# Rebuilding the first batch of a fused attention and Fourier-mixing kernel: order of transposes, loads and folds, and one mixing product over all channels

## The chip, the cores and the metric

The kernel runs on one core of one Trainium2 chip. The metric is the device time of one launch in microseconds (us). Before the change it took 1139.79 us, the median of three runs (1139.76 to 1141.58 us); the profiled execution spans 1140.0 us from its first to its last instruction. Where a moment is given below, it is counted from the start of that span. The engines are TensorE (PE; PEld is its weight load), VectorE (DVE), ScalarE (ACT), GpSimd (POOL) and SyncE (SP), which here only issues transfers.

## What is computed

There are 8 batches, 8 heads, 576 tokens and a head width of 64. Attention is local to chunks of 64 tokens. Its output, laid out as 576 x 512 for each batch, goes through a Fourier mix over tokens and channels, a normalization and a two-layer MLP (512 to 2048 to 512).

```python
def _attn_ref(q, k, v):                       # 8 x 8 x 576 x 64, chunk = 64
    scores = scale * np.matmul(q_c, k_c.transpose(0, 1, 2, 4, 3))
    scores = scores - np.max(scores, axis=-1, keepdims=True)
    attn = np.exp(scores)
    attn = attn / (np.sum(attn, axis=-1, keepdims=True) + 1e-09)
    return np.matmul(attn, v_c)

def _moe_ref(x, w_ch1, w_ch2):                # x: 8 x 576 x 512
    X = np.fft.fft(x, axis=1)
    X = np.fft.fft(X, axis=2)
    u = x + np.real(X).astype(np.float32)
    mu = np.mean(u, axis=-1, keepdims=True)
    var = np.mean((u - mu) ** 2, axis=-1, keepdims=True)
    un = (u - mu) / np.sqrt(var + 1e-06)
    return u + np.maximum(un @ w_ch1, 0.0) @ w_ch2
```

The two weight matrices arrive as float64 and are turned into float32 on the chip, piece by piece (32 pieces of 128 x 512).

## The kernel before

A batch's nine chunks make four tiles of 128 tokens and half a tile. "LO" tiles hold chunks from the front, "HI" tiles chunks from the back in mirrored order, and "RE" (rest) tiles hold the middle chunks of two batches. Token n and token 576 - n share their Fourier factors, so a LO and a HI tile are **folded**: their sums and differences are taken over tokens and then over channels, which quarters the Fourier products. For this the LO tiles are shifted by one row across tile borders (`shift`). The Fourier transform is then two matrix products with cosine and sine tables: `z` over the tokens, `mix` over the channels.

The first batch has nothing before it to hide behind, so it has its own code. The MLP of group 0 can start when the four tiles of batch 0 are normalized and transposed; from then on the MLPs of all groups follow each other on PE, and the next batches' attention, the rounding of the weights (`round_weight`) and a conversion of the second weight matrix (`keep2`) are woven in between the MLP's steps.

The order of the first batch's work (cut):

```python
def attention_early():
    def ready(n):
        for i in range(NM):                   # NM = 2
            if n == at[LO, 0, i]: shift_early(i)
            if n == at[HI, 0, i]: fold(0, i)  # on VectorE
        if n == at[LO, 0, 0]: fold(0, NM)     # the rest tile, on GpSimd
        if n + 3 > hi: load_v(n + 3)
    att_T(lo)                                 # q, k transposed by PE, copied by ACT
    for n in range(lo, hi + 1):               # 5 tiles: RE, LO 0, LO 1, HI 0, HI 1
        att_S(n)                              # scores on PE; max, subtract (DVE); exp (ACT)
        if n > lo:
            att_V(n - 1)                      # product with v, scaled by DVE
            ready(n - 1)
        if n < hi:
            att_T(n + 1)
        yield
        att_P(n)                              # probabilities transposed; sums, reciprocal
        yield
    att_V(hi)
    ready(hi)
    yield
```

The fold of one pair, the rounding of one piece, and the main program's beginning (all cut):

```python
def fold(b, i):
    eng = nc.vector if b < 2 and (b, i) != (0, NM) else nc.gpsimd
    ...                                       # for a pair: sum of two tiles 128x512,
    ...                                       # four adds or subtracts 128x256, two small copies

def round_weight(i):
    if i < len(pieces):                       # first half of piece i
        nc.vector.tensor_scalar(wi, hi, 0x000FFFFF, None, ALU.bitwise_and)
        nc.scalar.activation(out=w, in_=wi, func=ACTF.Copy, scale=2.0 ** -20, bias=1.0)
        nc.vector.tensor_scalar(p, hi, 0x7FF00000, None, ALU.bitwise_and)
        nc.scalar.activation(out=p, in_=p, func=ACTF.Relu, scale=-1.0, bias=top[:, 0:1])
        nc.scalar.activation(out=p, in_=p, func=ACTF.Relu, scale=-8.0, bias=top[:, 1:2])
    if 0 < i <= len(pieces):                  # second half of piece i - 1
        nc.vector.scalar_tensor_tensor(w, lo, 2.0 ** -52, w, ALU.mult, ALU.add)
        nc.vector.scalar_tensor_tensor(p, hi, 0x80000000, p, ALU.bitwise_and, ALU.bitwise_or)
        nc.vector.tensor_tensor(out=w, in0=w, in1=p.bitcast(FP32), op=ALU.mult)

# main
for n in range(3): load(n); load_v(n)         # q, k and v of tiles 0 to 2
for n in range(3, first[1]): load(n)
for n in range(3, first[1]): load_v(n)
for i in range(len(spaces)): load_weight(i)   # 7 pieces of the weights
for step, _ in enumerate(attention_early()):
    if step == 0:
        load_tables()                         # issued by GpSimd
        load_dim_tables()
    if step == 6:
        turn_tables()                         # copies on GpSimd
    keep_warm(1)                              # idle matmuls, 2 instructions each
keep_warm(5)
for step, _ in enumerate(fourier(0)):
    for _ in range((2, 1, 0)[step]):
        round_next()
...
for g in range(NG):                           # the MLPs
    for _ in mlp(g):
        ...                                   # due steps of the next batch's attention
        if not heavy:
            round_next()
            if t <= 4 or t % 4 == 0:
                round_next()
        for _ in range(2 if n_w <= len(pieces) else 3):
            if n_w > N_LAST + 2 and n_conv < 5 or n_w > len(pieces):
                n_conv += 1
                next(conv2, None)             # a step of keep2, mostly one DVE operation
```

In `fourier(0)` the token products are taken for one pair of quarters after the other, each over both tile pairs and the rest; the channel product `mix` covers half of the channels and its mirror half is made by two VectorE operations a tile (`both`) from a copy that ACT makes.

Of the kernel before, what the change touches and what calls it, by code (L numbers as in the profile page):

```python
# [16 lines left out]
def kernel(  # L17
# [94 lines left out]

    LO, HI, RE = "lo", "hi", "rest"
    tiles, first = [], []
    for b in range(B):
        first.append(len(tiles))
        if b % 2 == 0:
            tiles.append((RE, b, 0))
        tiles += [(what, b, i) for what in (LO, HI) for i in range(NM)]
# [37 lines left out]
    es, rs, pT = {}, {}, {}  # L157
# [3 lines left out]
    dims = [start[:, d0 + o:d0 + o + n_] for o, n_ in ((0, HM + 1), (HM + 1, HM - 1), (2 * HM, HM + 1), (3 * HM + 1, HM - 1))]  # L161
# [53 lines left out]
    def load_tables():  # L215
# [5 lines left out]
        for c in range(2 * NM):  # L221
            (i, r0), (j, p0) = divmod(c * CH, 128), divmod((NC - 1 - c) * CH, 128)
            nc.gpsimd.dma_start(out=t[r0:r0 + CH, i], in_=seq_tab[p0:p0 + CH, j])
        for r0 in (0, CH):
            nc.gpsimd.dma_start(out=t[r0:r0 + 1, NM], in_=seq_tab[0:1, 0])
            nc.gpsimd.dma_start(out=t[r0 + 1:r0 + CH, NM], in_=seq_tab[1:CH, NM])

    def load_dim_tables():
        nc.gpsimd.dma_start(out=dims[0], in_=dim_tab[:, 0, 0:HM + 1])
        nc.gpsimd.dma_start(out=dims[1], in_=dim_tab[:, 2, 1:HM])  # L230
        nc.gpsimd.dma_start(out=dims[2][0:1], in_=dim_tab[0:1, 1, 0:HM + 1])
        nc.gpsimd.dma_start(out=dims[3][0:1], in_=dim_tab[0:1, 3, 1:HM])

    def turn_tables():
        t = start[:, 0:(NM + 1) * 2 * NQ]
        a, b = tk.rearrange("p i r f -> p (i r) f"), t.rearrange("p (i f) -> p i f", f=NQ)
        for c in range(2 * NM):
            nc.gpsimd.tensor_copy(a[:, :, c * CH:(c + 1) * CH], b[:, :, (c + 1) * CH:c * CH:-1])
        nc.gpsimd.tensor_copy(a[:, :, NL:NL + 1], b[:, :, 0:1])
        nc.gpsimd.tensor_copy(a[:, :, NL + 1:NQ], b[:, :, NL + 1:NQ])  # L240
        nc.gpsimd.memset(cx[:, 0:HQ + 1], 0.0)
        nc.gpsimd.tensor_copy(ce, dims[0][:, ::2])
        nc.gpsimd.tensor_copy(co, dims[0][:, 1::2])
        nc.gpsimd.tensor_copy(so, dims[1][:, ::2])
        nc.gpsimd.tensor_copy(so[0:1], dims[3][0:1, ::2])
        nc.gpsimd.tensor_copy(cx[:, HQ + 1:HM], dims[1][:, 1::2])
        nc.gpsimd.memset(cx[0:1, HQ + 1:HM], 0.0)
        nc.gpsimd.tensor_copy(cx[0:1, 0:HQ + 1], dims[2][0:1, ::2])
# [58 lines left out]
    def att_T(n):  # L307
# [24 lines left out]
        if low and n == at[LO, 0, 1]:  # L332
# [12 lines left out]
    def att_S(n):  # L345
        a, b = qT.pop(n), kT.pop(n)
        sc = ps_a.tile([128, 2, 512], FP32, tag="att", name="sc")
        for j in range(NJ):
            for e in range(2):
                for c in range(2):  # L350
# [7 lines left out]
                    )  # L358
        s4 = sc[:, :, 0:NJ * CH].rearrange("p e (j k) -> p e j k", j=NJ)
# [24 lines left out]
    def att_V(n):  # L384
# [35 lines left out]
        if kind(n) == HI:  # L420
            nc.gpsimd.tensor_copy(x[:, 0:1], x[:, DM:DM + 1])
# [3 lines left out]
    def shift_early(i):  # L425

        lows = [xt(at[LO, 0, j])[:, 0:DM] for j in range(NM)]
        rest = xt(rests[0])[0:1, 0:DM]
        if i == 0:
            nc.gpsimd.tensor_copy(first_rest[CH:CH + 1, 0:DM], rest)  # L430
            nc.gpsimd.tensor_copy(rest, lows[0][0:1])
            nc.gpsimd.tensor_copy(lows[0][0:1], lows[0][CH:CH + 1])
        else:
            nc.scalar.copy(lows[0][CH:CH + 1], lows[1][0:1])
            nc.scalar.copy(lows[1][0:1], lows[1][CH:CH + 1])
            nc.scalar.copy(lows[1][CH:CH + 1], first_rest[CH:CH + 1, 0:DM])
# [15 lines left out]
    def fold(b, i):  # L452

        eng = nc.vector if b < 2 and (b, i) != (0, NM) else nc.gpsimd
        two = one_p.tile([128, 2 * (HM + 1)], FP32, tag="two", name="two")
        if i < NM:
# [3 lines left out]
            nc.gpsimd.memset(s[:, DM:DM + 1], 0.0)  # L460
# [27 lines left out]
    def attention_early():  # L488
# [3 lines left out]
        def ready(n):  # L492
            for i in range(NM):
                if n == at[LO, 0, i]:
                    shift_early(i)
                if n == at[HI, 0, i]:
                    fold(0, i)
            if n == at[LO, 0, 0]:
                fold(0, NM)
            if n + 3 > hi:  # L500
# [3 lines left out]
        for n in range(lo, hi + 1):  # L504
            att_S(n)
            if n > lo:
                att_V(n - 1)
                ready(n - 1)
            if n < hi:
                att_T(n + 1)  # L510
            yield
            att_P(n)
            yield
# [626 lines left out]
```

## Time and profile before

| | before |
|---|---|
| time, median of 3 | 1139.79 us |
| PE busy | 1093.8 us (96% of the span) |
| DVE busy | 599.2 us (53%) |
| ACT busy | 290.3 us (25%) |
| POOL busy | 274.3 us (24%) |
| read from HBM | 166.96 MB |
| first matmul of the first MLP | 65.10 us |

Busy times overlap, so they do not add up to the span. "L303" is line 303 of the kernel. In a line of the timeline the first number is the start and the second the duration; in brackets stands how long the engine sat idle before it, and after the arrow whose work ended that idle time. In the view by windows, each engine's busy time stands with the number of its instructions, then the TensorE clock granted as a share of full speed, the busy share of the 16 DMA engines and the GB/s that they moved. The matmuls are float32, and each one that the program asks for shows as two instructions.

### The profile page before, as it was taken

How to read it: one execution, taken by the hardware profiler on the slowest of the kernel's cores; microseconds unless marked ns; L12 is line 12 of the kernel's file. 1: busy time of each engine (PE TensorE's matmuls, PEld its weight loads, DVE VectorE, ACT ScalarE, POOL GpSimd, SP SyncE). 2: the span in 40 equal slices, each digit the busy share in tenths (PEclk: the TensorE clock that was granted, in tenths of full speed). 3: DMA queues.
4: the chain of work that ended last, by engine and by line, in shares of the span. 5: the costliest groups of instructions: out<-in, count | busy, mean ns of one | idle time of the engine just before them, and what ended most of it. 6: DMA issues, size and time to landing. Idle time of an engine off the chain costs nothing. (4 is left out here: it accounts for less than half of the span.)

```text
span 1140.0 us, 18688 instructions
## 1 busy us (share of the span) xinstructions
PE 1093.8 (96%) x7040; PEld 846.3 (74%) x7040; DVE 599.2 (53%) x1241; ACT 290.3 (25%) x711; POOL 274.3 (24%) x406
## 2 busy tenths in 40 slices
PE   5789998999999999999999999899999999999998
PEld 4544444445888888778888888788888888888887
DVE  4699978524356445563556365654555434423521
ACT  3577652121202221222113211321032202201210
POOL 4100101336400531043305140063015400130140
PEclk9999998999999999999999999999999999999999
DMA  9737652787556725773466546662664246446332
GB/s 172 221 96 210 177 175 72 225 262 234 211 168 188 234 96 181 230 198 118 165 209 173 176 140 203 179 206 111 187 203 125 84 161 197 128 145 214 94 108 77
DMA packets 150123, 192.47 MB, mean 169 GB/s; under 512 B 68820, under 2 KB 106713, under 8 KB 142865
## 3 DMA queue, kind: packets, MB, share of 16 engines
q1 hardware_dynamic: 147184, 189.57, 54.7%
q0 software_dynamic: 704, 1.17, 0.5%
q8 instruction: 56, 0.92, 0.3%
q10 hardware_dynamic: 2144, 0.52, 0.3%
q14 instruction: 35, 0.28, 0.1%
HBM read 166.96 MB, written 24.12 MB: 168 GB/s over the span
## 5 line engine op out<-in xcount | busy, mean ns | idle before, releaser
L791 POOL TENSOR_TENSOR h<-h 128x256 f32<-128x256 f32 x64 | 55.4, 871 | 415.6 <-PE pb L885 303.3
L932 PE MATMUL pa<-wb,h 128*128 128x256 f32 x512 | 116.1, 381 | 0.0
L932 PE MATMUL pb<-wb,h 128*128 128x256 f32 x512 | 115.0, 381 | 0.0
L885 PE MATMUL pb<-unT,wa 128*128 128x256 f32 x448 | 106.7, 381 | 4.4 <-DVE wa L894 4.4
L885 PE MATMUL pb<-wa 128*128 128x256 f32 x448 | 107.1, 382 | 0.8 <-DMA wa<-s 0.6
L885 PE MATMUL pa<-unT,wa 128*128 128x256 f32 x448 | 107.8, 383 | 0.0
L932 PEld LDWEIGHTS pa<-wb,h 128*128 128x128 f32 x512 | 95.8, 190 | 14.6 <-issue 1.6
L932 PEld LDWEIGHTS pb<-wb,h 128*128 128x128 f32 x512 | 95.8, 190 | 12.9
L885 PEld LDWEIGHTS pb<-unT,wa 128*128 128x128 f32 x448 | 84.2, 190 | 18.9 <-DVE wa L894 7.6
L885 PEld LDWEIGHTS pb<-wa 128*128 128x128 f32 x448 | 83.5, 190 | 13.7 <-DVE wa L892 1.2
L885 PEld LDWEIGHTS pa<-unT,wa 128*128 128x128 f32 x448 | 83.2, 190 | 11.6
L900 ACT ACTIVATE h<-pa 128x256 f32<-128x256 f32 x56 | 21.5, 384 | 176.2 <-PE pa L885 143.2
L839 PE MATMUL dn<-wb,h 128*128 128x512 f32 x128 | 60.6, 623 | 1.9 <-ACT h L809 1.9
L801 PE MATMUL up<-unT,wa 128*128 128x512 f32 x128 | 58.0, 599 | 1.7 <-ACT h L809 0.9
L892 DVE TENSOR_TENSOR wa<-pa,wa 128x256 f32<-128x256 f32 x56 | 23.8, 425 | 66.5 <-PE pa L885 62.9
L932 PE MATMUL pa<-wb,yall 128*128 128x256 f32 x256 | 58.2, 382 | 0.0
L885 PE MATMUL pa<-wa 128*128 128x256 f32 x224 | 54.0, 384 | 3.8 <-ACT wa L890 3.8
L818 PE MATMUL up<-unT,wa 128*128 128x512 f32 x128 | 57.5, 598 | 0.0
L932 PE MATMUL pb<-wb,yall 128*128 128x256 f32 x256 | 57.1, 380 | 0.0
L932 PE MATMUL pb<-wb 128*128 128x256 f32 x256 | 56.6, 379 | 0.0
L932 PEld LDWEIGHTS pb<-wb 128*128 128x128 f32 x256 | 48.2, 190 | 6.3
L636 POOL TENSOR_TENSOR xall<-y,xall 128x513 f32<-128x513 f32 x14 | 21.3, 1522 | 131.1 <-DVE y L630 131.1
(211 smaller groups left out, 1698.5 us busy)
## 6 DMA issues: line engine op xcount, KB each, us to landing
wb<-s SPq DMA_DIRECT2D x56, 1024.0 KB
wa<-s SPq DMA_DIRECT2D x196, 256.0 KB
xall<-in_moe_w_ch_dram SPq DMA_DIRECT2D x22, 512.0 KB
q<-in_q_dram SPq DMA_DIRECT2D x96, 112.0 KB
k<-in_k_dram SPq DMA_DIRECT2D x96, 112.0 KB
v<-in_v_dram SPq DMA_DIRECT2D x132, 64.0 KB
yall<-in_moe_w_ch_dram SPq DMA_DIRECT2D x10, 512.0 KB
s<-wb SPq DMA_DIRECT2D x20, 256.0 KB
```

Source lines behind the costliest of these rows:

```text
L636: eng.tensor_tensor(out=x[:, 0:w], in0=y[:, 0:w], in1=x[:, 0:w], op=ALU.add)
L791: nc.gpsimd.tensor_tensor(out=h1[:, m, hi], in0=h1[:, m, lo], in1=h1[:, m, hi], op=ALU.subtract)
L801: nc.tensor.matmul(out=up, lhsT=w1[:, kk, m * 128:(m + 1) * 128], rhs=unT[:, kk], start=(kk == 0), stop=(kk == KD - 1),)
L818: nc.tensor.matmul(out=up, lhsT=w1[:, kk, m * 128:(m + 1) * 128], rhs=unT[:, kk], start=(kk == 0), stop=(kk == KD - 1),)
L839: nc.tensor.matmul(out=dn, lhsT=h1[:, m, s * 128:(s + 1) * 128], rhs=w2[:, m, :], start=(m == 0), stop=(m == KF - 1),)
L885: nc.tensor.matmul(out=dst, lhsT=w[:, kk, r], rhs=rhs[o][:, kk], start=(o in (0, 2) and kk == 0), stop=(kk == 1), skip_group_check=True,)
L892: nc.vector.tensor_tensor(out=b, in0=dst, in1=a, op=ALU.add)
L900: nc.scalar.activation(out=h1[:, m, lo], in_=dst, func=ACTF.Relu)
L932: nc.tensor.matmul(out=dst, lhsT=lhs[:, m], rhs=w[:, m], start=(o in (0, 2) and m == 0), stop=(m == HF - 1), skip_group_check=True,)
```

## The change

It rebuilds only what happens before the first MLP, and alters the pace of one conversion after it.

- **Order of the tiles.** RE, LO 1, HI 1, LO 0, HI 0, so that the pair 1 is complete two tiles before the end.
- **Transposes ahead of the softmax.** The transposes of the next tile's q and k come right after the scores; maximum, subtraction and exp follow them.
- **Loads in order of use.** All of q and k go ahead of most of v; the tables follow v in the queue of SyncE rather than being issued by GpSimd. The channel tables are now loaded at full width, the sine table as rows 1 to 127, with row 0 assembled from two other rows.
- **One pair folded by GpSimd.** Pair 1 goes to GpSimd, pair 0 stays on VectorE; the token tables are turned by ACT.
- **Its products first.** The token products run pair 1, pair 0, rest, all four quarters of each, with idle matmuls between them.
- **Mix at all channels.** The channel product covers all 512 columns for batch 0, and VectorE adds it straight from PSUM, so the copy and the two mirroring operations fall away.
- **Rounding.** Two calls instead of three come before the first MLP, one of them at its very end; `keep2` goes at two steps a turn instead of three.

The diff, cut:

```diff
-        tiles += [(what, b, i) for what in (LO, HI) for i in range(NM)]
+        tiles += [(LO, 0, 1), (HI, 0, 1), (LO, 0, 0), (HI, 0, 0)] if b == 0 else [ ... ]
...
-            nc.gpsimd.dma_start(out=t[r0:r0 + CH, i], in_=seq_tab[p0:p0 + CH, j])
+            nc.sync.dma_start(out=t[r0:r0 + CH, i], in_=seq_tab[p0:p0 + CH, j])
...
     def load_dim_tables():
-        nc.gpsimd.dma_start(out=dims[0], in_=dim_tab[:, 0, 0:HM + 1])
-        nc.gpsimd.dma_start(out=dims[1], in_=dim_tab[:, 2, 1:HM])
...
+        nc.sync.dma_start(out=cos_d, in_=dim_tab[:, 0, :])
+        nc.sync.dma_start(out=sin_d[1:128], in_=dim_tab[1:128, 2, :])
+        for i in range(2):
+            nc.sync.dma_start(out=first_rest[32 + 32 * i:33 + 32 * i, 0:DM], in_=dim_tab[0:1, 1 + 2 * i, :])
+
+    def turn_dim_row():
+        for i in range(2):
+            nc.gpsimd.tensor_copy(sin_d[0:1, i::2], first_rest[32 + 32 * i:33 + 32 * i, i:DM:2])
...
-            nc.gpsimd.tensor_copy(a[:, :, c * CH:(c + 1) * CH], b[:, :, (c + 1) * CH:c * CH:-1])
+            nc.scalar.copy(a[:, :, c * CH:(c + 1) * CH], b[:, :, (c + 1) * CH:c * CH:-1])
...                                            # shift_early in three steps, two on GpSimd, one on ACT
-        eng = nc.vector if b < 2 and (b, i) != (0, NM) else nc.gpsimd
+        eng = nc.vector if (b, i) == (0, 0) or b == 1 else nc.gpsimd
...
         for n in range(lo, hi + 1):
             att_S(n)
+            if n < hi:
+                att_T(n + 1)
+            softmax(n)
             if n > lo:
                 att_V(n - 1)
                 ready(n - 1)
-            if n < hi:
-                att_T(n + 1)
             yield
             att_P(n)
             yield
+        shift_early(2)
+        turn_tables()
         att_V(hi)
         ready(hi)
...
+    def fourier_early():
+        order = (1, 0, NM)
+        for i in order:
+            for T in range(4):
+                nc.tensor.matmul(out=z[T][:, 0:NQ], lhsT=pm[i][p, d0_:d0_ + HQ], rhs=tk[p, i, T // 2], **at_)
+            ...                                # four one-row products for the middle channel
+            if i != order[-1]:
+                keep_warm(2)
+        ...                                    # z copied to zf by ACT and DVE in turn, zr by ACT
+        yield
+        for i in range(NM):
+            for T, tab in ((0, cos_d), (1, cos_d), (3, sin_d), (2, sin_d)):
+                nc.tensor.matmul(out=early_xp[0][i][:, T % 2::2], lhsT=zf[:, T, 128 * i:128 * (i + 1)],
+                                 rhs=tab[:, T % 2::2], start=(T == 0), stop=(T == 2), ...)
+        keep_warm(4)
+        yield
+        for i in range(NM):
+            y, (low, high) = early_xp[0][i], groups[0][2 * i:2 * i + 2]
+            x = xt(low)
+            nc.vector.tensor_tensor(out=x[:, 0:DM], in0=y, in1=x[:, 0:DM], op=ALU.add)
+            means([low])
+            ...                                # the same for high; then as before
+            if i > 0:
+                normed(0, 1)
+                turned_(1)
+            normed(0, 2 * i)
+            means([high])
+            turned_(2 * i)
+        normed(0, 3)
+        turned_(3)
+        yield
...
+        for what, n in (
+            (load, 0), (load, 1), (load_v, 0), (load, 2), (load_v, 1), (load, 3), (load, 4),
+            (load_v, 2), (load_v, 3), (load_v, 4),
+        ):
+            what(n)
+        load_tables()
+        load_dim_tables()
         for i in range(len(spaces)):
             load_weight(i)
...
         for step, _ in enumerate(attention_early()):
-            if step == 0:
-                load_tables()
-                load_dim_tables()
-            if step == 6:
-                turn_tables()
-            keep_warm(1)
-        keep_warm(5)
-        for step, _ in enumerate(fourier(0)):
-            for _ in range((2, 1, 0)[step]):
+            keep_warm((step + 1) % 2)
+        turn_dim_row()
+        for step, _ in enumerate(fourier_early()):
+            if step == 0:
+                turn_dim_tables()
+            if step != 1:
                 round_next()
...
-                for _ in range(2 if n_w <= len(pieces) else 3):
+                for _ in range(2):
```

## The prediction, made before the changed kernel was run

> **What bounds the kernel now.** I read the page first: busy shares, then the slices of the span.
>
> ```profile
> PE   5789998999999999999999999899999999999998
> DVE  4699978524356445563556365654555434423521
> PEclk9999998999999999999999999999999999999999
> ```
>
> From the third slice on PE is full; only the first two slices (28.5 us each) are loose. So the kernel is bound by PE once the MLPs run, and what can be won lies ahead of the first MLP matmul. The timeline gives that moment, and the two later places where PE stops:
>
> ```profile
> 23.68 0.63 PE L303 MATMUL pt<-ident,start 128*128 128x128 f32 x4 [2.03 <-DMA start<-in_k_dram]
> 28.50 0.63 PE L303 MATMUL pt<-ident,start 128*128 128x128 f32 x4 [1.10 <-DMA start<-in_k_dram]
> 65.10 1.12 PE L801 MATMUL up<-unT,wa 128*128 128x512 f32 x2 [0.67 <-ACT unT L709]
> ...
> 134.25 5.40 PE L839 MATMUL dn<-wb,h 128*128 128x512 f32 x8 [1.90 <-ACT h L809]
> ...
> 195.51 1.08 PE L303 MATMUL pt<-ident,un 128*128 128x128 f32 x4 [5.63 <-DVE un L696]
> ```
>
> The first MLP starts at 65.10 us. Before it the transposes of late tiles wait for k: at 23.68 and 28.50 us a load ends the wait. Later PE stands 1.90 us for ACT and 5.63 us for DVE, both because DVE is behind with rounding weights. The view by windows shows what the stops cost besides:
>
> ```profile
> 134.00:138.00 4.00, 3.75 (x5) 1.65 (x6) 3.50 (x11) 1.66 (x4) 0.22 (x2) 0.59 0.81 179
> 138.00:142.00 4.00, 4.00 (x13) 1.91 (x12) 3.81 (x12) 1.39 (x3) 0.00 (x0) 0.99 0.21 48
> ...
> 195.50:199.50 4.00, 3.99 (x11) 2.75 (x12) 3.97 (x6) 1.17 (x2) 0.20 (x1) 0.50 0.40 113
> ```
>
> The number after POOL's is the granted clock: after a stop PE ran at 0.59 and 0.50 for 4 us, a loss of some 2 us each. From 65.10 us to the end stand 1074.9 us, nearly all matmuls that the change leaves alone. The time after is therefore the new start of the first MLP plus about 1074.9 us, corrected for what the change does to those two stops.
>
> **What the Trainium skill says.**
> - "TensorE: Matmul & The Clock Gate", Part 1 (the HAM clock gate): about 3.4 us of idleness halves PE's clock, and as much activity restores it. The 0.50 after 5.63 us agrees; here already 1.90 us of standstill had that effect.
> - "DMA: Bandwidth & Descriptors", "Why a DMA increments its semaphore by 16 and not by 1": a transfer is spread over the largest number of engines up to 16 that divides its row count; 127 rows go to one engine. The new sine load has 127 rows. No transfer in the trace of before has that shape, so nothing here confirms it yet.
> - "SBUF — State Buffer", "Who interferes with whom": a DVE operation with two SBUF inputs and a GpSimd operation that reads SBUF exclude each other. The trace agrees in part: DVE's add at L636, 128x512, averages 898 ns over 20, against 692 ns for the same shape at L461; POOL runs its share of L636 beside it.
>
> **The change part by part.** Durations are those of before.
>
> *Period of a tile.* In before, scores of tile 1 start at 15.45 us and of tile 2 at 19.90: 4.45 us. In it exp (0.63) stands in ACT's queue ahead of the copies qT and kT (0.58 and 0.60), for which the next scores wait. With the transposes first, PE does scores (0.46 to issue) and eight transposes (1.1), ACT copies q and k by 2.36 us after the scores' start, while DVE needs 0.76 + 0.73 + 0.69 = 2.18 for maximum and subtraction. Exp runs 2.36 to 2.99, the probabilities' transposes 3.06 to 3.5, then the next scores: 3.55 us a tile, 0.9 less.
>
> *Loads.* All 16 DMA engines are full until 28 us, at some 190 GB/s with rows of 256 B (the windows view: 177 to 219). Each tile of q, k or v is 256 KB, 1.4 us. In before, five tiles of q and k, three of v and the tables (1.15 MB) compete, and the last k ends its wait at 28.50 us. In the new order 3.07 MB stand before and with the last k: 2.5 us of start + 16.2 + some 2 us to land = 20.7 us. By the new period tile 4's transposes come at 22.3 us, so the loads no longer hold a tile. The two waits on k (3.1 us) go.
>
> *Last scores.* First scores at 9.80 as before (the first q lands at 7.18). Tile 1's transposes run from 10.9 on a cold PE (1.97 us), exp 0 is then behind kT, second scores at 14.65; three more periods give 25.4 us for tile 4. In before: 32.23 us. Gain 6.8 us.
>
> *Folds.* Pair 1 on GpSimd: rows of the view by form are
>
> ```profile
> L461 POOL TENSOR_TENSOR sum<-xall 128x512 f32<-128x512 f32 x12 | 15.5, 1295 | 3.8 <-DMA xall<-first 3.3
> L468 POOL TENSOR_TENSOR two<-sum 128x256 f32<-128x256 f32 x12 | 8.9, 739 | 0.9
> L461 DVE TENSOR_TENSOR sum<-xall 128x512 f32<-128x512 f32 x4 | 2.8, 692 | 0.8 <-POOL sum L460 0.6
> ```
>
> 1.30 + 0.74 + 0.25 + 0.64 + 0.69 + 0.71 + 0.24 and 0.3 for column copy and memset: 4.9 us, twice DVE's 2.8. Tile 2 is complete at 24.9, so it ends at 29.8. A row copy (0.6) follows, then the rest tile (3.7 as in before) until 34.1. ACT's two row copies (1.2) wait for GpSimd's row copy, so 30.4 to 31.6; then the token tables: four copies of 384 columns and two small ones, an estimate of 2.3 us from ACT's 0.59 for 512 columns: ready at 33.9. Pair 0 on DVE: last scores + 0.76 + 1.42 + exp 0.7 + transposes 0.7 + copy 0.7 + product 0.8 + scaling 0.8 gives 31.3; its sum waits for ACT's row at 31.6, 2.8 us more, and up to 2 us of exclusion against the rest fold: 34.4 to 36.5.
>
> *Token products.* 33.9 is the start for pair 1. A product is two instructions, 0.55 us in before (eight instructions in 2.22): four are 2.2, the one-row products 0.2, two idle matmuls 1.14; pair 0 the same; the rest 1.65. Sum 2.4 + 1.14 + 2.4 + 1.14 + 1.65 = 8.7, end at 42.6. PE has stood some 3 us before, so I add 1 us, half the cold loss: 43.6. In before this point was 47.8.
>
> *Sine table.* If one engine carries it: weights came in at 395 GB/s over 16 engines (window 34 to 36 us), 24.7 GB/s each, so 127 x 2048 B take 10.5 us. It starts after 5.0 MB of other loads, at about 28.5, and lands at 41 to 42: it is needed at 44.5. Hidden, with 2 to 3 us in hand. The first weights' part on that engine comes 1.3 us behind it, also in time for its rounding at about 44.
>
> *Mix and what follows.* Four products of 256 columns are 1.8 us a pair: DVE adds from 45.4 us. The chain on DVE (start of one to start of the next: add 0.73, statistics 0.83, un 0.46) is the one of before, 53.33 to 65.10 = 11.8 us, less four mirror operations (4 x 0.43), plus two one-column adds: 10.3, so transposed inputs at 55.7. But the second rounding call now stands behind the last un, and the first matmul needs piece 0, which that call completes: five DVE operations, 2.6 us behind un at 54.3. **First MLP matmul at 56.9; I take 57.0**, 8.1 us earlier.
>
> *Afterwards.* In before DVE had 1.5 us of lead over PE there (63.62 against 65.10) and one rounding call fewer left. Now it starts level. DVE is at 90% or more until 140 us, so the 1.90 us stop grows by 0 to 1.5: 0.7. For the 5.63 us stop I counted DVE's calls after the wait for the mix of batch 1 (173.43 us): one rounding more (2.6 us), four keep2 operations fewer (4 x 0.6 = 2.4). No change. PE's pause of about 2 us before the first matmul (transposes end at 55.0) may leave it cold: a third of 2 us, 0.6.
>
> Sum: 57.0 + 1074.9 + 0.7 + 0.6 = 1133.2 of span, and the timed runs lie 0.2 under the profiled span: **1133.0 us**.
>
> **Rivals.**
> 1. *The tables become the bound.* They are last in the queue, one on a single engine, and SyncE has over 40 transfers to issue at 0.6 us or more each. If they come 4 us later than I say, the mix waits, the weights behind them too, and the first MLP starts at 59 to 61: 1135 to 1137. For it: the issue of v took 7.96 us for eight transfers (21.90 us in the timeline). Against: 1.15 MB less competes earlier on.
> 2. *GpSimd becomes the bound.* Twice as slow, and with shift, fold 1, rest and row copies in one queue. If DVE and GpSimd exclude each other throughout, the products slip by 2 to 3 us: 1135 to 1136. Against: only pair 1 is needed first, the others have 3.5 and 7 us more.
> 3. *The gain is lost at the later stops.* DVE, not PE, sets the pace from 65 to 140 us; then an earlier start of PE only makes the stop at 132 us longer. Against: DVE starts earlier too, all but 1.5 us, as counted.
> 4. *All goes well*, PE stays warm and the stops do not grow: 1129 to 1131.
>
> **Range and chances.** The parts that are certain (waits on k, ACT's order, the mirror operations) make 8 to 10 us; the errors of start (2 us), DMA (3) and stops (2) add up to some 4. So 1133.0, 1128.5 to 1138.0 for 8 in 10. Two per cent is 22.8 us, more than a third of all the time before the first MLP: within 2% has 0.98, either side 0.01.
>
> **What the profile after would show.** Right: no wait of a transpose on q or k after the first; scores about 3.6 us apart, the last at 25 to 26; token products from 34, VectorE's first add near 45.4, the first matmul at 57, waiting for the second half of piece 0; stops near 124 us (2 to 3.5 us) and 181 us (5 to 6). Wrong: a wait of the mix on the sine table, of the first rounding on a weight, of the products on GpSimd's fold, a start after 60 us, or a stop of DVE's making over 8 us.

## The result: earlier start, same time

After the change the kernel takes **1141.82 us** (median of four runs, 1141.05 to 1143.53); before, in the same measurement, 1140.22 us (1139.76 to 1141.58). The ratio is 1.0014, its 95% interval 0.9997 to 1.0031: no difference that can be told from zero, where 7 us less had been predicted. The profiled executions span 1139.3 us after and 1140.0 before; a timed run of any kernel here is 1.7 to 1.9 us longer than its own span. The profiled execution of before was one of 1141.79 us, that of the changed kernel one of 1141.05.

The page after, by slices: the only loose slices are again the first two, and in sum nothing has moved.

```profile
PE   7799997998999999999999999899999999999998
DVE  4599978524356446553556365654555434423521
PEclk9999998999999999999999999999999999999999
```

So the averages do not tell where the gain went. The timeline of PE after the change does (cut; start, duration, and in brackets the idle time with what ended it):

```profile
36.06 2.12 PE L697 MATMUL z<-tk,pm 128*128 128x289 f32 x4 [3.63 <-POOL pm_rest L504]
60.02 10.54 PE L877 MATMUL up<-unT,wa 128*128 128x512 f32 x24 [1.57 <-DVE wa L303]
...
129.15 3.70 PE L915 MATMUL dn<-wb,h 128*128 128x512 f32 x8 [1.90 <-ACT h L885]
189.13 1.09 PE L313 MATMUL pt<-ident,un 128*128 128x128 f32 x4 [6.03 <-DVE un L772]
...
262.99 0.69 PE L409 MATMUL xp<-v,pT 64*64 64x64 f32 x32 [2.03 <-issue]
280.54 1.89 PE L601 MATMUL z<-tk,pm 128*128 128x289 f32 x6 [2.41 <-POOL pm L496]
```

The first MLP starts at 60.02 us in place of 65.10. At the end of the stop for un PE is even 6.4 us ahead of before (189.13 against 195.51): the 1.90 us stop near 130 us was followed by no loss of clock this time (1.00 from 128 to 136 us, where before had 0.59 after it). Then two stops follow that before did not have, or had at 0.7 us: attention of a later batch at 262.99 us (the view names no releaser; SyncE issued its v only from 258.60 to 261.43 us) and the token product `z` at 280.54 us, which waits for GpSimd's fold. After the stop at `z` the clock is lower, as the windows show (the number after POOL's is the granted clock):

```profile
280.00:284.00 4.00, 3.46 (x11) 1.94 (x12) 0.00 (x0) 0.28 (x2) 3.92 (x7) 0.75 0.70 138
284.00:288.00 4.00, 4.00 (x16) 3.40 (x16) 0.00 (x0) 0.74 (x6) 0.11 (x1) 0.83 0.60 156
```

At `z` the lead is down to 1.8 us (280.54 against 282.32), at the next token product to 0.2 (288.03 against 288.22). From the first MLP matmul to the end pass 1079.3 us, not the 1074.9 of before. Of these 4.4 us, 4.6 are lost between the un stop and `z` (91.4 us in place of 86.8) and 1.1 after it; 1.3 were won before.

Why is the fold late? GpSimd waits for the shift of batch 2, which is a set of transfers in SyncE's queue:

```profile
265.93 1.27 POOL L480 TENSOR_TENSOR sum<-xall 128x512 f32<-128x512 f32 x1 [2.62 <-DMA xall<-first]
```

The shift leaves the queue at 261.74 us, 201.7 us after the first MLP matmul; before, 198.5 us after it. This moment says more than the length of the stop. In all fifteen traces in which PE waits at `z` (of seventeen), the product goes on 18.6 to 19.0 us after the shift has left, whatever PE lost elsewhere. The queue, first before (cut), then after the change:

```profile
181.83 1.31 SPq L770 DMA_DIRECT2D s<-xall  x3
...
196.43 1.76 SPq L183 DMA_DIRECT2D q<-in_q_dram  x4
...
205.60 2.02 SPq L770 DMA_DIRECT2D s<-xall  x3
...
210.16 2.39 SPq L183 DMA_DIRECT2D q<-in_q_dram  x4
...
217.23 0.66 SPq L727 DMA_DIRECT2D out_dram<-o  x1
```

```profile
163.29 0.61 SPq L846 DMA_DIRECT2D s<-yall  x1
190.03 1.76 SPq L186 DMA_DIRECT2D q<-in_q_dram  x4
...
193.74 0.43 SPq L846 DMA_DIRECT2D s<-wb  x1
194.22 1.53 SPq L846 DMA_DIRECT2D s<-xall  x3
...
203.80 1.99 SPq L186 DMA_DIRECT2D q<-in_q_dram  x4
205.89 1.80 SPq L186 DMA_DIRECT2D k<-in_k_dram  x4
208.09 2.59 SPq L212 DMA_DIRECT2D v<-in_v_dram  x4
210.73 0.60 SPq L846 DMA_DIRECT2D s<-wb  x1
...
215.14 0.63 SPq L803 DMA_DIRECT2D out_dram<-o  x1
```

L770 and L846 are the stores of `keep2`, the conversion of the second weight matrix, seven of 256 KB for each of four quarters. After 163.9 us a load of q holds the queue for 26.1 us, because its buffer is free only when VectorE has read qT; behind it stand the stores of the second quarter. The fourth quarter (from 210.73) stands behind the loads of batch 3. Before, the second (181.83) and the fourth (205.60) went ahead of these loads. The change's last line, two steps of `keep2` a turn in place of three, is the suspect; the next runs test it.

### The profile page after: what moved, and what is told of

It reads as the page before. It is cut to its first block, busy times and chain, and to the rows that moved or that the text cites. A ratio compares the mean times of both kernels' runs of the same rounds, so it can differ in the third digit from the quotient of the medians.

```text
span 1139.3 us, 18658 instructions
## 1 busy us (share of the span) xinstructions
PE 1094.5 (96%) x7028; PEld 847.4 (74%) x7028; DVE 599.6 (53%) x1238; ACT 290.5 (25%) x708; POOL 272.7 (24%) x395
## 5 line engine op out<-in xcount | busy, mean ns | idle before, releaser
L961 PEld LDWEIGHTS pa<-unT,wa 128*128 128x128 f32 x448 | 83.2, 190 | 11.6
L1008 PEld LDWEIGHTS pa<-wb,yall 128*128 128x128 f32 x256 | 47.7, 190 | 6.9 <-issue 0.5
```

The costliest lines, as they stand in the source:

```text
L961: nc.tensor.matmul(out=dst, lhsT=w[:, kk, r], rhs=rhs[o][:, kk], start=(o in (0, 2) and kk == 0), stop=(kk == 1), skip_group_check=True,)
L1008: nc.tensor.matmul(out=dst, lhsT=lhs[:, m], rhs=w[:, m], start=(o in (0, 2) and m == 0), stop=(m == HF - 1), skip_group_check=True,)
```

## Experiments on the pace of keep2

Each was timed in five rounds beside the kernel before on the same chip (1140.32 to 1141.10 us).

**The old kernel at the new pace** (on the kernel before):

```diff
-                for _ in range(2 if n_w <= len(pieces) else 3):
+                for _ in range(2):
```

> The kernel before with the new pace of keep2 alone (two steps a turn). With three rounding calls ahead of the first MLP its rounding ends one turn earlier, so the stores of the second quarter still stand ahead of the loads. Theory A (order in the queue is what counts, and needs both the pace and the missing rounding call): no loss, and two VectorE operations fewer ahead of the stop, 1138.5 to 1140.5. Rival C (the slower pace as such costs the later stores their time): 1142 to 1144.

Measured: 1142.90 us, ratio 1.0017 (1.0008 to 1.0025). The pace costs about 2.6 us even without the rest of the change; a theory by which it costs nothing here falls. Its trace shows why: the second quarter does go out ahead of the load of q, as expected (180.49 against 193.26 us), but the fourth goes out behind the loads of batch 3 (212.47 us). The shift leaves 199.8 us after the first MLP matmul, and PE stops 2.2 us for v and 2.7 us at `z`.

**The changed kernel at the old pace** (the same line the other way round):

> The changed kernel with the old pace of keep2 (three steps a turn once all weights are rounded). Theory A: the stores come ahead of the loads as well, so PE's waits at 260 to 285 us go; but four more VectorE operations stand ahead of the normalization of the second group, so PE's stop for it (6.0 us in the changed kernel) grows by 1 to 2.5 us: 1138 to 1140. Rival B: only the longer stop is seen: 1142 to 1144.

Measured: 1137.04 us, ratio 0.9970 (0.9961 to 0.9979). The rebuilt first batch is worth 3.3 us, and the new pace costs the kernel 4.8. The queue of SyncE and the waits of PE from 186 to 290 us in this kernel:

```profile
163.58 0.67 SPq L846 DMA_DIRECT2D s<-wb  x1
185.88 1.30 SPq L846 DMA_DIRECT2D s<-xall  x3
...
199.03 0.68 SPq L846 DMA_DIRECT2D s<-wb  x1
199.80 2.06 SPq L846 DMA_DIRECT2D s<-xall  x3
...
204.81 1.92 SPq L186 DMA_DIRECT2D q<-in_q_dram  x4
...
211.41 0.62 SPq L803 DMA_DIRECT2D out_dram<-o  x1
```

```profile
PE pt L313 <- DVE un L772: 6.6, 1, 6.6
PE z L601 <- POOL pm L496: 0.4, 1, 0.4
```

The second quarter begins ahead of the long wait, the fourth (199.03) is ahead of the loads of batch 3, the outputs leave 3.7 us earlier, the shift leaves 197.1 us after the first MLP matmul, and of the two late stops 0.4 us remains. No clock is lost from 202 us on.

**Only the second quarter ahead:**

```diff
-                for _ in range(2):
+                for _ in range(3 if t == 26 else 2):
```

> The changed kernel, with one step of keep2 moved: at turn 26 of the MLP three steps are taken instead of two, so that the seven stores of the second quarter of the converted weights stand in SyncE's queue ahead of the next tile's loads of q and k and not behind them. Theory A (the gain is lost in SyncE's queue: after the change those stores stand behind a load that waits 26.1 us for a VectorE operation, so they are issued 12 us later than before, the queue is late by some 4 us from 215 us on, and PE waits 2.0 us for v and 2.4 us for a fold that waits for a shift): the first MLP starts at 60.0 as in the changed kernel, the stores are issued near 180 us, both waits of PE at 260 to 285 us fall under 1 us, and the time is 1137 to 1138.5. Rival B (the stage from 200 to 285 us is bound by the amount of transfers or by GpSimd's work, whatever its order): the waits stay and the time is 1141 to 1142.5.

Measured: 1140.96 us, ratio 1.0004 (0.9995 to 1.0014). The outputs are back in place (152.2 us after the first MLP matmul; before 152.1, changed kernel 155.1), but PE still stops 2.7 us at `z`, and its clock is 0.64 in the window from 280 to 284 us. The fourth quarter still goes out at 209.3 us, behind the loads. The stop at `z` is as long as it was for a plain reason: PE no longer stops for v, so it is there sooner. The product itself starts 217.6 us after the first MLP matmul and not 220.5, since the shift leaves at 198.6 and not 201.7.

**Only the last quarters sooner:**

```diff
-                for _ in range(2):
+                for _ in range(2 if t < 28 else 5):
```

> The changed kernel with keep2 at two steps a turn up to turn 27 and five a turn from turn 28 on, so that nothing is added ahead of the normalization of the second group, but the last two quarters' stores leave by turn 29 instead of 31, ahead of the loads of turn 30. Theory A2 (place of the last quarter in SyncE's queue): last keep2 store near 206 instead of 214, keep1's first store at 218 to 219.5, stop of PE for normalization still 6.0, 1136.5 to 1138.5. Rival E (what the old pace bought was something ahead of turn 28, such as the second quarter's early stores): 1140 to 1142.5.

Measured: 1142.62 us, ratio 1.0020 (1.0012 to 1.0029). The fourth quarter is now ahead of the loads of batch 3, but the second stands behind the 26-us wait, and the outputs leave 155.3 us after the first MLP matmul. PE stops 2.4 us for v, with a clock of 0.81 and 0.76 after it. The shift leaves as late as in the changed kernel, 201.6 us after the first MLP matmul.

**A first try at both** (`range(3 if t == 26 or t >= 28 else 2)`):

> The changed kernel with three steps of keep2 in turn 26 and from turn 28 on, two else: the second quarter of keep2's stores goes out ahead of the load that waits for qT, and the last two quarters come sooner. Theory P (the pace costs by both places: seven stores pushed behind the wait of 26 us in which the DMA engines stand idle, and the last quarter behind the loads of batch 3): the span looks like that of the changed kernel at the old pace, from the first MLP matmul to the end 1073 to 1074.5 us, pm of batch 2 at 205 us after that matmul, 1136.5 to 1138.5 us in all. Rival (something else in the slower pace costs, such as VectorE's order between turns 20 and 26): 1140 to 1142 us, as with each part alone.

Measured: 1141.00 us, ratio 1.0000 (0.9990 to 1.0010). A miss: at three steps a turn the fourth quarter (209.5 us) still goes out behind the loads of q and k of batch 3, so this edit does not put both ahead.

**Both ahead** (`range(3 if t == 26 else 2 if t < 28 else 5)`):

> The changed kernel with three steps of keep2 in turn 26, five from turn 28 on and two else: SyncE then issues all its transfers in exactly the order of the changed kernel at the old pace; VectorE does a few of keep2's subtractions later. Theory O (SyncE's order is the cost: with the fourth quarter behind the loads, or the second behind the wait of 26 us, the outputs, keep1's stores and the shift of batch 2 leave later): 1136.5 to 1138.5 us, from the first MLP matmul to the end 1073 to 1075.5 us, pm of batch 2 at 205 to 207 us after that matmul. Rival V (VectorE's order at turns 20 to 30 costs): 1140 to 1142 us, 1077 us or more from the first MLP matmul to the end.

Measured: **1136.94 us**, ratio 0.9966 (0.9956 to 0.9977): the whole cost of the pace is gone, though VectorE still does some of the subtractions later than at the old pace. SyncE's transfers stand in the same order as at the old pace. In its profile PE's stop for v is absent and the one at `z` is short, and no clock is lost there:

```profile
PE z L601 <- POOL pm L496: 0.7, 1, 0.7
```

```profile
280.00:284.00 4.00, 3.60 (x16) 2.48 (x17) 0.00 (x0) 1.02 (x6) 3.90 (x7) 1.00 0.71 129
284.00:288.00 4.00, 4.00 (x19) 3.35 (x18) 0.00 (x0) 0.37 (x1) 0.00 (x0) 1.00 0.93 293
```

SyncE's order is thus the cost, not VectorE's: the medians show that. This trace shows it less well than it seems. It belongs to the longest of the eight runs (a span of 1139.2 us, the first MLP at 63.04 us, because its tables landed late), and it lost clock after the 1.9 us stop near 130 us (0.57 from 132 to 136 us, some 1.7 us), which the trace with the second quarter alone ahead did not. So PE came to `z` that much later and stopped the less. Its shift leaves at 198.7 us after the first MLP matmul, no sooner than there (198.6); less the 1.7 us it would be 197.0, an estimate, where the old pace has it (197.1).

Nor is a lost clock what decides. Each half alone brings 1 us or nothing and both bring 4.9, and in the traces with one half left the clock fell after the stop that remained (2.4 or 2.7 us). But in the old kernel at the new pace stops of 2.2 and 2.7 us were followed by 1.00 throughout, and the pace cost it 2.6 us all the same.

**Is it the queue or the traffic?** Two runs moved stores of the changed kernel from SyncE to GpSimd, first the 28 of `keep2`, then the 28 of `keep1` (the same conversion of the first matrix, from 222 us on):

```diff
-            nc.sync.dma_start(out=to[o, :, m:m + 2], in_=a)          # keep2
+            nc.gpsimd.dma_start(out=to[o, :, m:m + 2], in_=a)
```

> The changed kernel with keep2's 28 stores issued by GpSimd's queue instead of SyncE's; its pace (two steps a turn) stays. Theory A2 (the last quarter's stores, at the slow pace, stand in SyncE's queue directly ahead of the first group's output stores, of keep1's stores and of the loads and shifts behind them; the queue, not the amount of traffic, is late): SyncE reaches the output stores as soon as PE has finished them, near 210.5 us, keep1's first store at 217 to 218.5, PE's waits at 260 to 285 us fall under 1 us, 1136 to 1138. Rival B (traffic of the DMA engines, or GpSimd's own chain): keep1's stores stay near 222 and the time is 1140.5 to 1143.

Measured: 1138.12 us, ratio 0.9980 (0.9972 to 0.9988). The second quarter still left no sooner than 195 us, now behind a wait of GpSimd; but loads no longer stand behind stores, the stop for v is gone, the one at `z` is 1.5 us, and the shift leaves 199.3 us after the first MLP matmul.

```diff
-            nc.sync.dma_start(out=to[:, :, o, kk], in_=a.rearrange("p (a x) -> p a x", a=2))    # keep1
+            nc.gpsimd.dma_start(out=to[:, :, o, kk], in_=a.rearrange("p (a x) -> p a x", a=2))
```

> The changed kernel with the 28 stores of keep1 issued by GpSimd in place of SyncE; the slow pace of keep2 stays. Theory Q (SyncE's queue): in all ten traces so far the span ends 875.9 to 878.5 us after the shift of batch 2 leaves SyncE's queue, and from the end of its wait at 186 to 190 us to that shift the queue works off 98 transfers at 0.72 to 0.74 us. With 28 fewer ahead of it the shift goes some 20 us earlier and is no longer the bound: the waits of PE on the late v load (2.0 us) and on GpSimd's pm at the mix (2.4 us) vanish, from the first MLP matmul to the end pass 1073 to 1075 us in place of 1079.3, 1135 to 1138 us in all. Rival D (the slower pace costs through the later work on VectorE and GpSimd itself, not through the queue): the two waits stay and the time stays at 1140 to 1142 us.

Measured: **1147.83 us**, ratio 1.0063 (1.0051 to 1.0075), outside both expectations. With 28 transfers fewer ahead of it the shift left SyncE hardly sooner (263.68 us, 201.1 after the first MLP matmul; 201.7 in the changed kernel). VectorE waited for a load of q, and PE for VectorE:

```profile
DVE qT L330 <- DMA q<-in_q_dram: 20.5, 2, 18.4
```

```profile
PE sc L362 <- DVE xall L428: 8.3, 1, 8.3
```

So the number of transfers in SyncE's queue is not the bound by itself, and my theory of 98 transfers at 0.73 us falls in that form. The windows of the changed kernel show what it left out:

```profile
164.00:190.00 26.00, 19.97 (x101) 10.88 (x101) 21.23 (x41) 7.75 (x20) 3.36 (x2) 0.93 0.11 42
190.00:262.00 72.00, 70.49 (x426) 33.73 (x424) 33.69 (x54) 14.06 (x24) 22.50 (x22) 0.98 0.86 255
```

From 190 to 262 us the 16 DMA engines are 86% busy (80% at the old pace), while in the 26 us ahead they do next to nothing: 0.11, against 0.26 at the old pace. What is not sent before 190 us is sent in a stretch with little room, whoever issues it. That these shares are the cause is argued and not shown: with both quarters ahead it is 0.27 and then 0.84. The Trainium skill has in "Trainium Kernel Development and Optimization", Key Constraints, that transfers issued by SyncE, ScalarE and GpSimd run on the same 16 DMA engines, and that a second issuer saves only time of issue. The two runs do not contradict it: with `keep2` on GpSimd the loads gained a place in the order of issue, with `keep1` there the same engines carried both streams. In the latter run SyncE issued the q that was waited for from 237.75 us on, 6.7 us later than the changed kernel (231.04), behind an output store that waited for VectorE; q was read at 253.11. The k behind it waited 7.2 us for output stores to land, while from 225 to 262 us GpSimd's queue carried 5.60 of 9.23 MB. That the output stores, slowed by these, held q is likely and not shown.

## Experiments on the first batch

The start fell short of 57.0 us by 3.0. The rest of the runs looks for that, most at the old pace.

**Sine table with 128 rows** (row 0 is overwritten later, as in the changed kernel), at the new pace:

```diff
-        nc.sync.dma_start(out=sin_d[1:128], in_=dim_tab[1:128, 2, :])
+        nc.sync.dma_start(out=sin_d, in_=dim_tab[:, 2, :])
```

> The changed kernel with the sine table loaded as 128 rows instead of rows 1 to 127; row 0 is overwritten afterwards as it was assembled before. If the 127 rows went over one DMA engine, the stretch of about 25 GB/s at 33.5 to 36.5 us is gone, the 2048-byte packets take under 2 us in place of 14, and GpSimd's two row copies run near 36 us instead of 46.3. Theory: the table was hidden behind the products all the same, so the first MLP starts at 59.5 to 60.0 and the time is 1141 to 1142. Rival D (the table or the weights behind it bound the start): the start moves to 57 to 58.5; the time moves only if the later stage lets it.

Measured: 1142.11 us, ratio 1.0012 (1.0003 to 1.0022), first MLP matmul at 60.00 us: neither moved. But the traffic did. The same window, first in the changed kernel and then with 128 rows (the last two columns are DMA share and GB/s):

```profile
33.50:36.50 3.00, 0.44 (x1) 0.36 (x2) 2.24 (x7) 2.12 (x6) 1.64 (x4) 0.95 0.07 26
```

```profile
33.50:36.50 3.00, 1.09 (x2) 0.83 (x3) 1.18 (x4) 1.81 (x6) 2.24 (x8) 0.50 0.87 213
```

127 rows did go through one engine, at 26 GB/s (a DMA share of 0.07, about one in 16); 128 rows and the weights behind them flow at 213. GpSimd's copies of the row that is assembled start at 34.85 us in place of 46.31.

**Idle matmuls while PE waits for the tables** (old pace):

```diff
-            keep_warm((step + 1) % 2)
+            keep_warm(7 if step == 10 else (step + 1) % 2)
```

> The changed kernel with the old pace of keep2 (1137.0 by itself) and six more idle matmuls in the gap between the last product with v and the token products, about 3.6 us of PE work. Theory W (the products of the first pair ran at half clock after 3.6 us of standstill, which cost 2 us): the four products of pair 1 take 2.2 us instead of 4.1, the first MLP starts at 57.7 to 58.3 instead of 60.0, and the time is 1134.5 to 1136. Rival: VectorE's and ScalarE's chain sets the start, PE's speed there is hidden: start 59.5 or later and 1136.5 to 1138.

Measured: 1138.51 us, ratio 0.9982 (0.9971 to 0.9993): no better than without them (1137.04). The token products took 8.1 us in place of the 9.8 of the changed kernel, and the mix then stood for the row of the sine table:

```profile
49.27 2.99 PE L727 MATMUL early_xp<-start,zf 128*128 128x256 f32 x12 [2.38 <-POOL start L240]
```

**Sine table alone at the old pace**, the missing cell of a two by two:

> The changed kernel with the old pace and the sine table of 128 rows, without the idle matmuls. Theory J (PE's cold clock at the token products and the sine table on one engine lie behind each other, so each remedy alone brings nothing): the same as the changed kernel at the old pace, 1136.5 to 1138 us, first MLP matmul 24 to 24.7 us after ACT's copies of the token tables. Rival (the idle matmuls are worth nothing, the table is all): 1134 to 1135.5 us, as the kernel with both, and 22 us after the copies.

Measured: 1137.11 us, ratio 0.9963 (0.9951 to 0.9974): the same as at the old pace without it. The first MLP matmul comes 24.9 us after the copies; the first four products are still cold (2.27 + 2.13 us).

**Both together:**

> The changed kernel with the old pace, the sine table loaded with 128 rows, and seven idle matmuls at the last step of the attention of batch 0. Theory J (two bounds lie behind each other): each remedy alone moved nothing, since with idle matmuls alone the mix then waited 2.4 us for the sine row, and with 128 rows alone PE was still cold; together the first MLP matmul comes 22.1 us after ACT has copied the token tables (24.1 to 25.3 in the runs so far without both), that is at 57.5 to 59.5 us by when the tables land, and the time is 1133 to 1136 us. Rival (the DVE chain or the weights set the start): still 24 us or more after the tables, 60 us or later, 1137 to 1139 us.

Measured: **1134.95 us**, ratio 0.9956 (0.9939 to 0.9973). The first MLP matmul comes at 58.10 us, 22.5 us after the copies of the token tables, where the traces so far without both need 24.1 to 25.3: products at full clock (1.14 us for each pair), and no wait for the row of the sine table. So in the start each remedy was hidden by the other's cost. In the total this run alone does not prove it: with six runs from 1132.86 to 1140.00 us its interval overlaps those of the single remedies. It lies 6.2 us under the kernel before on its chip, the old pace without remedies 3.3, and the two kernels below that also carry both remedies lie 6.6 and 6.5 under.

**Both rounding calls ahead of the mix** (old pace, 128 rows):

```diff
+        for _ in range(2):
+            round_next()
         for step, _ in enumerate(fourier_early()):
             if step == 0:
                 turn_dim_tables()
-            if step != 1:
-                round_next()
```

> The changed kernel with the old pace of keep2, the sine table as 128 rows (so that the weights land 7 to 9 us earlier), and both rounding calls placed ahead of the token products, where VectorE idles 9.6 us. Theory: piece 0 is ready long before the first MLP, whose wait of 1.6 us for it goes; start at 58.2 to 58.7; VectorE enters the MLP 1.5 us ahead instead of level, and its stop at 189 us (6.6 us at this pace) falls to 4.5 to 6; 1133.5 to 1135.8. Rival: a weight lands too late and holds the copies of the products back: start at 60 or later, 1137 or more.

Measured: 1136.94 us, ratio 0.9966 (0.9954 to 0.9979). The first matmul no longer waits for piece 0 (0.7 us for ACT remain), and it comes 23.2 us after the tables' copies (24.9 with the table of 128 rows alone), but the total is that of the old pace alone.

**Sequence tables issued by GpSimd at 13 us**, as before the change, on top of both remedies:

> As the joint kernel, and the eight transfers of the sequence tables are issued by GpSimd at the third step, at about 13 to 17 us, as the kernel before did. Theory T (the tables are late because SyncE first issues twelve transfers of v at some 0.7 us each): the tables have landed before ACT is done with the row copies, so the copies of the tables begin at 32.3 to 32.6 us in place of 33.2 to 35.7, and scatter less; first MLP matmul at 56.5 to 58, 1131.5 to 1134 us. Rival (bandwidth): the earlier tables delay the last k by some 3 us, scores of tile 4 at 28 to 29 in place of 26.4, and the start is no earlier than in the joint kernel.

Measured: 1134.49 us, ratio 0.9943 (0.9930 to 0.9956), 0.5 us from the run without, which is within the noise. ACT no longer waits for the tables, but the scores of the last tile come at 28.15 us, not 25.46 as in the run without, and the first MLP matmul at 59.31 us, not 58.10. That is what the rival said: tables that come earlier hold up q and k, whose loads compete with them.

**All of it** (both remedies, tables on GpSimd, early rounding calls):

> As the kernel with the tables on GpSimd, and both first rounding calls ahead of the mix of batch 0. The wait of the first MLP matmul for the second half of piece 0 (1.6 us) goes: start at 55 to 57 us. If the first MLP's start carries through, 1130 to 1132.5 us. If VectorE's later stops or SyncE's queue take it back, as in the run with the early roundings (start to end 1075.2 in place of 1073.1), 1132 to 1134.5 us, with the shift of batch 2 no earlier than in the kernel with the tables on GpSimd.

Measured: 1134.60 us, ratio 0.9946 (0.9934 to 0.9958); its profiled run had the first MLP at 60.80 us and not at the 55 to 57 expected, since q, k and v came late, though only 21.7 us after the tables' copies. Nothing is added in the total. These two kernels and the joint one lie 6.2 to 6.6 us under the kernel before on the same chip.

One table puts start and remainder side by side, from single profiled executions. "Outputs" is the moment at which the first output store leaves SyncE, "fold" the one at which GpSimd's first folded quarters of batch 2 are ready, both counted from the first MLP matmul:

| kernel | first MLP | outputs | fold | to the end | median us |
|---|---|---|---|---|---|
| before | 65.10 | 152.1 | 206.5 | 1074.9 | 1140.22 |
| changed | 60.02 | 155.1 | 210.0 | 1079.3 | 1141.82 |
| before, new pace | 65.43 | 151.6 | 208.0 | 1076.1 | 1142.90 |
| changed, old pace | 59.86 | 151.5 | 205.1 | 1073.1 | 1137.04 |
| last quarters sooner | 62.22 | 155.3 | 209.6 | 1079.3 | 1142.62 |
| both quarters ahead | 63.04 | 152.9 | 206.7 | 1076.2 | 1136.94 |
| old pace, sine table of 128 rows | 61.12 | 153.5 | 207.1 | 1075.8 | 1137.11 |
| joint remedies, old pace | 58.10 | 151.3 | 205.0 | 1073.0 | 1134.95 |

The later the fold, the longer the remainder. But single executions scatter: the two kernels at the old pace that differ only by the sine table are 2.7 us apart in the remainder, at the same median. Of this 1.7 us are clock: a stop of 1.9 to 2.0 us near 130 us is in all seventeen traces, and in eight of them the clock is down after it (0.57 in one window of 4 us, or some 0.8 in two). The profiles of the changed kernel, of the old pace and of the joint remedies are also the shortest executions of their kernels. The medians, not this table, give the sizes.

The starts of the eight kernels with the same first batch lie between 59.86 and 63.04 us, 24.1 to 25.3 us after the copies of the token tables, which end between 35.6 and 38.0 us by when the tables land. Their mean is 61.7 us: 3.6 us earlier than the two starts without the rebuild (65.10 and 65.43), which fits the 3.3 us of the medians better than the 5.1 us of one pair of profiles.

## Why the prediction was wrong

**What bounds the kernel** was read rightly up to 190 us, and too narrowly after it. The step that failed is the sentence that the 1074.9 us after the start are "nearly all matmuls that the change leaves alone". The diff's pace of `keep2` lies in that stretch. Under *Afterwards* its operations were counted on VectorE (four fewer by the stop for un, "no change") and not its stores in SyncE's queue. Measured: 1079.3 us at the new pace, 1073.1 at the old in the profiled executions, and 4.8 us between the medians.

**The sum.** The prediction lies 8.8 us under the median. In its own terms: the start came 3.0 us later (60.02 for 57.0); the remainder was 1079.3 us and not the 1076.2 to which the two corrections bring it (3.1); the timed run is 1.75 us longer than its span and not 0.2 shorter (1.95); and the profiled run is 0.8 us under the median. The third item is a slip of reading: the span of before came from an execution of 1141.79 us and was set beside a median of 1139.79 of others.

**Afterwards, the stops that were counted.** The first grew by 0, not 0.7 (1.90 us both times); the second by 0.4 (6.03 against 5.63). PE's pause before the first matmul left no cold start. Rival 3, the gain lost at later stops, came true, but at other stops: v and `z`, after 260 us, made by transfers and not by VectorE's rounding. Rival 1 named the start that came (59 to 61) and its cause, late tables, but neither the mix nor the weights waited in the changed kernel.

**Period and last scores** were right in mechanism: no transpose waits for k, from the second on the scores lie 3.6 to 4.0 us apart, and the last start at 26.36 us (25.4 predicted).

**Folds and tables**: the tables were ready at 35.96 us (33.9). GpSimd had folded pair 1 by 30.5 us, and ACT's row copies ended at 32.33 (31.6), so 0.7 us came down the chain of the scores. The other 1.5 us are ACT's wait for the tables, for which the sum has no term: it let all loads flow at 190 GB/s. SyncE issued the twelve last transfers of v, 64 KB each, from 17.09 to 25.95 us, at 89 GB/s, and only then the tables. The run with another queue shows that this order alone was not to blame: the same bytes earlier hold up k. The view names `pm_rest` as what ended PE's wait of 3.63 us, but GpSimd's last write to it ended at 35.35 us, and ACT's last copy of the tables at 35.96, 0.1 us ahead of the product. Rival 2 did not come: beside GpSimd's rest fold VectorE's fold of pair 0 took 3.2 us, not 2.8 (its first add 0.99 us, not 0.69), and nothing waited for it.

**Token products**: the cold PE cost 1.8 us (the first four products took 2.12 + 1.96 us, not 1.14 each pair), not 1. The windows view has it at 0.57 from 36 to 40 us after an idle time of 3.63 us. "TensorE: Matmul & The Clock Gate", Part 1, in the Trainium skill names about 3.4 us of idleness for that; here a stop of 2.41 us at `z` was followed by 0.75 and 0.83. Cold start included, the products took 10.0 us to the start of the mix (9.7 predicted): at full clock they are half a microsecond shorter than the sum had them (8.2 us in the joint run).

**Sine table**: one engine, as "DMA: Bandwidth & Descriptors", "Why a DMA increments its semaphore by 16 and not by 1", had it, now with 26 GB/s beside it. The single rows behind it reached GpSimd at 46.31 us (41 to 42 predicted for the table): just hidden in the profile of the changed kernel, 2.38 us too late with a warm PE.

**Mix and what follows**: first add at 48.43 us (45.4), then 11.6 us to the first matmul, as predicted, with the wait for the second half of piece 0 (1.57 us) as foreseen. So the 3.0 us of the start are 2.2 us of tables (products from 36.06 us for 33.9), 0.3 of products and 0.6 of the mix's first pair (2.4 us from its start at 46.03 to the first add, 1.8 predicted). The tables could come 2 us later still, as the eight starts show.

**Open**: what of the 4.8 us each late transfer makes, since the one trace with both quarters ahead is of a long run; when a stop of about 2 us is followed by a lower clock; and whether the output stores held q for 18 us in the run with `keep1` on GpSimd.

## What to carry to other kernels

A change to how often background work is stepped is a change to the order of an in-order queue: list, for each queue, what now stands behind which wait, before calling the rest of the kernel unchanged. A stretch in which the DMA engines idle behind one waiting load (here 0.11 busy) is the place to try for stores, above all when the stretch after it is full (0.86). And where two waits hide behind each other, or a stop of 2 us brings a cold clock on top, remedies have to be tried together; alone each looked worthless here. Last, profiles of single executions of one kernel differ by as much as the effect looked for: compare moments inside a trace with what ended the wait, and totals by medians.

## What had not been expected of the hardware

- A stop of 2.41 us at `z` was followed by a granted clock of 0.75 and 0.83 in the two windows of 4 us there, one of 2.7 us at the same place in the old kernel at the new pace by 1.00, and the same stop of 1.9 to 2.0 us near 130 us by a lower clock in eight of seventeen traces.
- A transfer of 127 rows of 2048 bytes ran at 26 GB/s and two single rows issued behind it were ready for GpSimd at 46.31 us; with 128 rows, in a stretch at 213 GB/s, at 34.85 us.
- Moving 28 stores of 256 KB from SyncE's queue to GpSimd's cost 6.0 us for one matrix (`keep1`) and gained 3.7 us for the other (`keep2`), by the medians against the changed kernel.
